# Linear attention with a gated convolution: batch 7's product of k and v moved next to the second half of batch 6's attention

## The chip, the cores and the metric

The kernel runs on one core of a Trainium2 chip. A core has a matrix engine (TensorE; PE in the rows, with its weight loads as PEld), VectorE (DVE), ScalarE (ACT), GpSimd (POOL), and SyncE (SP), from whose queue all transfers are issued here. Each engine works through its own queue in order; semaphores hold an instruction until what it reads is there and what it overwrites has been read. The metric is the time of one execution on the device, in microseconds, as the median of several runs.

## What is computed

For 8 batches of 576 tokens and 8 heads of 64 channels (512 channels in all), linear attention and then a gated convolution:

```python
q_s = exp(q - max(q, -1));  q_s = q_s / (sum(q_s, -1) + 1e-9)   # over a head's channels
k_s = exp(k - max(k, 2));   k_s = k_s / (sum(k_s, 2) + 1e-9)    # over tokens
kv = einsum('bhsd,bhse->bhde', k_s, v)
x = einsum('bhsd,bhde->bhse', q_s, kv)                          # heads side by side: 512 channels
gate = sigmoid(sum(conv_w[j] * shifted(x, 4 - j) for j in range(5)))
out = (gate * (x @ w_val)) @ w_out
```

## The kernel before

The 512 channels are four blocks of 128 partitions, and a block of one batch is a tile of 128 x 576. Each batch goes through the same steps. In the names, the first number is the batch and the second the block, and a letter says which engine does the step (a ScalarE, v VectorE, p GpSimd).

- Keys: `load_k` (SP), the maximum over tokens by `k_peak` (VectorE) from a copy in another layout (`load_km`), a way through DRAM that spreads it over the partitions (`k_row`, `k_spread`, both SP), then `k_sub b 0` to `b 4` subtract it and `k_exp`, `kt_exp` (ScalarE) take the exponential. `kv b` is 80 small matmuls; `kv_sums` and `kv_norm` (VectorE) divide by the sums.
- Queries: `q_max`, `q_sub`, `q_exp`, `q_total`, `q_log`, `l_turn` give the logarithm of the sum; `l_row` and `l_spread` (SP) send it through DRAM into the tile lb; `l_sub` subtracts it from the queries (qc) in the layout by channels and `c_exp` (ScalarE) gives the normalised queries.
- `attend b 0` and `attend b 1` are 8 + 8 matmuls each, and give blocks 0, 1 and 2, 3 of x in PSUM.
- Gate: `first` multiplies x by the last tap, `tap` (VectorE) adds another tap straight from PSUM, `far` (ScalarE) with `near` (GpSimd) does the same in two steps, `sigmoid` (ScalarE) is a tanh of half the sum.
- Products in float32 are made of two parts in the format fp32r, a high and a low one: `x_high`, `x_low` split x, and `g_high`, `g_low` split the gated value. `value b m` and `project b n` are then 24 matmuls each (three products, four blocks, two halves of the tokens). `gated` (VectorE) multiplies gate and value, `copy` takes a finished block out of PSUM (halved, by one or two engines), `put` (SP) sends it out.

What sets the order is the table `ORDER`, a list of steps written out in full; the loop at the end of the kernel issues them one by one, and each engine's queue is the table with the other engines' steps left out. The batches overlap: while the products of batch 5 run, the keys and queries of batches 6 and 7 are made ready. `HOMES` is a table beside it that says which buffer each new tile takes; its row `bank` is that of the four PSUM banks of the wide tiles (x, val, out, kv).

Of the kernel before, what the change touches and what calls it, by code (L numbers as in the profile page):

```python
# [90 lines left out]
    near 3 0 0, q_sub 5 0 p, near 3 1 0, x_low 3 2, load_k 5, load_qc 4 2, q_sub 5 3 p, tap 3 2 0, tap 3 3 2,
    load_v 7, copy 2 3 a a, far 3 2 1, l_sub 4 1 p, tap 3 2 2, kt_exp 4, value 3 0, far 3 3 1, sigmoid 3 1,
    load_km 7 0, q_exp 5 0 4, l_sub 4 0 p, value 3 1, near 3 2 1, sigmoid 3 0, tap 3 3 3, gated 3 0, k_spread 5,
    l_sub 4 3 p, kv 4, c_exp 4 1, q_total 5, g_high 3 0 a, load_km 7 1, put 2 2, c_exp 4 0, g_low 3 0 p, value 3 2,
    gated 3 1, load_q 6 0 5, near 3 3 1, kv_sums 4, q_log 5, load_v 5, kv_norm 4 v, load_qc 5 2, l_turn 5,
    sigmoid 3 2, value 3 3, tap 3 3 0, l_row 5, put 2 3, gated 3 2, sigmoid 3 3, g_high 3 2 a, g_high 3 1 p,
    g_low 3 1 p, k_sub 5 3 p, g_low 3 2 p, attend 4 0, gated 3 3, k_peak 7 0, g_high 3 3 a, x_high 4 0 v, load_qc 5 3,
    g_low 3 3 p, project 3 0, first 4 0 v, c_exp 4 3, tap 4 0 3, l_sub 4 2 p, far 4 1 1, load_km 7 3, tap 4 0 2,
    project 3 3, k_sub 5 0 p, tap 4 0 1, copy 3 0 a a, first 4 1 a, put 3 0, q_max 6 0 5, k_sub 5 4 p, l_spread 5,
    far 4 1 0, c_exp 4 2, k_sub 5 1 p, x_high 4 1 a, kt_exp 5, project 3 1, copy 3 3 a a, x_low 4 0, q_sub 6 2 p,  # L100
    tap 4 0 0, put 3 3, load_qc 5 0, k_sub 5 2 p, tap 4 1 3, tap 4 1 2, attend 4 1, x_low 4 1, copy 3 1 a a,
    near 4 1 1, k_exp 5, k_peak 7 3, project 3 2, q_sub 6 3 p, x_high 4 3 a, x_high 4 2 v, first 4 2 v, near 4 1 0,
    tap 4 2 3, first 4 3 a, tap 4 3 3, q_sub 6 4 p, x_low 4 2, sigmoid 4 0, q_sub 6 0 p, x_low 4 3, value 4 0,
    sigmoid 4 1, tap 4 3 2, q_sub 6 1 p, copy 3 2 a a, tap 4 2 2, put 3 2, l_sub 5 1 p, load_qc 6 1, kv 5, load_kt 6,
    gated 4 0, q_exp 6 0 5, k_row 6, l_sub 5 0 p, load_k 7, tap 4 2 1, g_high 4 0 p, value 4 2, c_exp 5 1, kv_sums 5,
    g_low 4 0 p, tap 4 2 0, c_exp 5 0, load_qc 6 0, kv_norm 5 v, load_km 7 2, k_peak 7 1, l_sub 5 3 p, load_k 6,
    k_spread 6, tap 4 3 1, sigmoid 4 2, tap 4 3 0, attend 5 0, gated 4 2, value 4 1, l_sub 5 2 v, first 5 1 a,
    load_q 7 0 5, x_high 5 0 a, tap 5 1 3, load_v 6, sigmoid 4 3, tap 5 1 2, g_high 4 2 v, tap 5 1 1, g_low 4 2 p,
    value 4 3, gated 4 1, x_high 5 1 a, g_high 4 1 p, x_low 5 1, tap 5 1 0, g_low 4 1 p, c_exp 5 2, c_exp 5 3,
    gated 4 3, first 5 0 a, far 5 0 3, g_high 4 3 a, g_low 4 3 v, project 4 0, far 5 0 0, near 5 0 3, near 5 0 0,  # L110
    q_total 6, attend 5 1, copy 4 0 a a, k_sub 6 1 p, put 4 0, project 4 2, load_qc 7 2, x_high 5 3 a, k_sub 6 2 p,
    tap 5 0 2, load_qc 6 3, first 5 2 a, put 3 1, x_low 5 0, far 5 2 3, tap 5 0 1, near 5 2 3, q_max 7 0 4,
    project 4 1, q_log 6, far 5 2 2, copy 4 2 a a, first 5 3 a, l_turn 6, q_sub 7 1 p, x_high 5 2 a, q_sub 7 0 p,
    x_low 5 3, l_row 6, copy 4 1 a a, x_low 5 2, value 5 1, q_sub 7 3 p, tap 5 3 3, q_sub 7 2 p, k_peak 7 2,
    sigmoid 5 1, l_spread 6, tap 5 3 2, sigmoid 5 0, near 5 2 2, project 4 3, gated 5 1, put 4 2, k_row 7,
# [5 lines left out]
    project 5 2, x_high 6 1 a, c_exp 6 3, l_row 7, k_sub 7 4 p, first 6 1 a, x_high 6 0 a, tap 6 1 3, k_sub 7 0 p,
    first 6 0 a, project 5 0, copy 5 2 a a, l_sub 6 2 v, kt_exp 7, put 5 2, l_spread 7, tap 6 0 3, k_sub 7 1 p,
    tap 6 0 2, k_sub 7 3 p, project 5 1, tap 6 0 1, copy 5 0 a a, c_exp 6 2, x_low 6 0, put 5 0, near 6 0 0,
    tap 6 1 2, tap 6 1 1, tap 6 1 0, attend 6 1, copy 5 1 a a, put 5 1, project 5 3, load_qc 7 0, x_high 6 2 a,
    x_high 6 3 v, far 6 2 2, k_sub 7 2 v, first 6 3 a, x_low 6 1, x_low 6 2, l_sub 7 3 p, x_low 6 3, value 6 1,
    sigmoid 6 1, tap 6 3 3, copy 5 3 a a, first 6 2 v, sigmoid 6 0, put 5 3, tap 6 2 3, near 6 2 2, k_exp 7,
    value 6 3, gated 6 1, l_sub 7 2 p, tap 6 3 2, tap 6 3 1, l_sub 7 1 p, tap 6 3 0, value 6 0, sigmoid 6 3,
    g_high 6 1 p, gated 6 3, g_low 6 1 p, tap 6 2 1, c_exp 7 2, tap 6 2 0, g_high 6 3 p, c_exp 7 1, l_sub 7 0 p, kv 7,
    sigmoid 6 2, value 6 2, kv_sums 7, kv_norm 7 v, c_exp 7 0, gated 6 0, g_low 6 3 v, g_high 6 0 a, g_low 6 0 p,
    attend 7 0, gated 6 2, g_high 6 2 a, x_high 7 1 v, first 7 0 a, g_low 6 2 p, project 6 1, c_exp 7 3, tap 7 0 3,  # L130
# [673 lines left out]
```

## Time and profile before

| | before |
|---|---|
| time, median of 3 runs | 287.67 us (287.59 to 287.77) |
| profiled execution: time | 287.65 us |
| profiled execution: span of the trace | 285.9 us |
| TensorE busy (matmuls) | 278.8 us, 98% |
| VectorE busy | 231.7 us, 81% |
| GpSimd busy | 205.8 us, 72% |
| ScalarE busy | 192.8 us, 67% |

The page names the share of each engine over the whole span. The windows say the same for a stretch: a row that gives as much busy time for TensorE as the stretch is long has no gap on TensorE in it. The chain of waits follows the work that ended last back from the end; pieces of the same engine that stand end to end in it have no wait between them. In the timeline the time in square brackets is how long an engine stood idle before the row, and what it waited for. A duration in a group of rows is a mean over the instructions of one line and one form.

### The profile page before, as it was taken

To read this page: it belongs to the slowest core of one execution; us is meant where nothing else is said; L and a number is where in the kernel's file an instruction comes from. 1 tells how busy PE (TensorE), PEld (TensorE's weight loads), DVE (VectorE), ACT (ScalarE), POOL (GpSimd) and SP (SyncE) were. 2 spreads that over 40 slices of the span, in tenths; PEclk is the share of its full clock that TensorE was granted. 3 is DMA by queue.
4 is the path that set the end of the run, shared out by engine and by line. 5 is a ranking of instruction groups with operands and counts; after the bars stand their busy time and mean duration, and the time that the engine had idled before them with its cause. 6 is when DMAs were issued, how large, how long until landed. Compare 5 with 4: busy or idle time off the path is not lost.

```text
span 285.9 us, 6653 instructions
## 1 busy us (share of the span) xinstructions
PE 278.8 (98%) x2640; PEld 250.6 (88%) x2640; DVE 231.7 (81%) x329; ACT 192.8 (67%) x322; POOL 205.8 (72%) x191
## 2 busy tenths in 40 slices
...
GB/s 241 397 414 399 316 226 301 214 416 346 84 262 345 250 284 128 332 198 224 371 417 257 211 225 322 287 165 126 153 182 159 217 0 2 44 41 85 0 83 85
DMA packets 23463, 62.93 MB, mean 220 GB/s; under 512 B 3432, under 2 KB 3976, under 8 KB 20744
## 3 DMA queue, kind: packets, MB, share of 16 engines
...
q14 instruction: 10, 0.08, 0.1%
HBM read 52.96 MB, written 9.54 MB: 219 GB/s over the span
## 4 chain that ended last, share of the span: by engine, by line
PE 84%; DVE 7%; ACT 2%; issue 1%; POOL 1%; DVEq 0%
PE val L630 36%; PE out_a L630 32%; PE kv L521 6%; PE x L580 5%; PE cv L676 2%; DVE gate L605 2%; DVE x L600 1%; PE qTps L546 1%; DVE e L292 1%; DVE kpk L340 1%; PE kps L387 1%; ACT q L506 1%; PE out_r L630 1%; PE out_l L630 1%; POOL f L295 0%
## 5 line engine op out<-in xcount | busy, mean ns | idle before, releaser
L630 PE MATMUL val<-x,w_val_hi 128*128 128x288 f32 x512 | 89.1, 295 | 0.1
L605 DVE SCALAR_TENSOR_TENSOR gate<-x,cw,gate 128x575 f32<-128x575 f32 (+3 forms) x98 | 78.8, 809 | 5.7 <-ACT gate L593 2.2
L630 PEld LDWEIGHTS val<-x,w_val_hi 128*128 128x128 f32 x512 | 75.3, 188 | 0.3 <-DVE x L600 0.3
L630 PE MATMUL val<-x,w_val_lo 128*128 128x288 f32 x256 | 56.1, 300 | 0.0
L630 PE MATMUL out_a<-gh,w_out_lo 128*128 128x288 f32 x248 | 54.6, 301 | 0.0
L630 PE MATMUL out_a<-gh,w_out_hi 128*128 128x288 f32 x248 | 53.2, 296 | 0.0
L697 POOL TENSOR_TENSOR gl<-g,gh 128x576 fp32r<-128x576 f32 x24 | 34.6, 1443 | 14.7 <-ACT gh L198 8.0
L630 PEld LDWEIGHTS out_a<-gh,w_out_lo 128*128 128x128 f32 x248 | 39.4, 188 | 5.7 <-issue 1.8
L630 PE MATMUL out_a<-gl,w_out_hi 128*128 128x288 f32 x248 | 43.0, 295 | 0.0
L614 POOL TENSOR_TENSOR gate<-gate,far 128x572 f32<-128x572 f32 (+3 forms) x22 | 29.1, 1324 | 18.7 <-DVE gate L605 10.0
L630 PEld LDWEIGHTS val<-x,w_val_lo 128*128 128x128 f32 x256 | 40.7, 188 | 1.6 <-DVE g L689 0.4
L630 PEld LDWEIGHTS out_a<-gh,w_out_hi 128*128 128x128 f32 x248 | 39.8, 188 | 0.0
L204 ACT ACTIVATE o<-out_a 128x576 f32<-128x576 f32 x27 | 17.6, 650 | 31.6 <-PE out_a L630 22.0
L630 PEld LDWEIGHTS out_a<-gl,w_out_hi 128*128 128x128 f32 x248 | 36.4, 188 | 0.0
L420 POOL TENSOR_TENSOR q<-q,qm 128x512 f32<-128x512 f32 x32 | 33.5, 1062 | 3.6 <-DVE qm L415 3.5
L689 DVE SCALAR_TENSOR_TENSOR g<-gate,val 128x576 f32<-128x576 f32 x32 | 23.8, 749 | 13.8 <-PE val L630 5.9
L490 POOL TENSOR_TENSOR qc<-qc,lb 128x576 f32<-128x576 f32 (+1 forms) x17 | 24.1, 1428 | 11.0 <-DMA lb<-lrow 11.0
L355 POOL TENSOR_TENSOR k<-k,kmax 128x512 f32<-128x512 f32 x23 | 30.2, 1330 | 0.2
L617 ACT ACTIVATE gate<-gate 128x576 f32<-128x576 f32 x30 | 20.2, 683 | 8.3 <-DVE gate L605 8.0
L600 DVE TENSOR_TENSOR x<-x,x 128x576 fp32r<-128x576 f32 x32 | 23.1, 749 | 1.7 <-ACT x L198 1.6
L610 ACT ACTIVATE far<-x,cw 128x572 f32<-128x572 f32 (+3 forms) x22 | 16.2, 737 | 9.2 <-PE x L580 4.0
L424 ACT ACTIVATE q<-q 128x512 f32<-128x512 f32 (+2 forms) x11 | 15.9, 1442 | 8.8 <-POOL q L420 8.8
...
## 6 DMA issues: line engine op xcount, KB each, us to landing
out<-o SPq DMA_DIRECT2D x31, 288.0 KB, 4.8
...
q<-in_q SPq DMA_DIRECT2D x7, 1024.0 KB, 10.5
km<-in_k_strided SPq DMA_DIRECT2D x24, 288.0 KB, 4.5
k<-in_k SPq DMA_DIRECT2D x6, 1024.0 KB, 7.4
qc<-in_q_channels SPq DMA_DIRECT2D x16, 288.0 KB, 5.0
...
kc<-in_k_channels SPq DMA_DIRECT2D x8, 288.0 KB, 8.5
```

What stands on the lines that cost most here:

```text
L204: nc.scalar.mul(out, in_, factor)
L355: engine(e).tensor_sub(kk[r, cs], kk[r, cs], mx[r, cs])
L420: engine(e).tensor_tensor(qq, qq, m, op=ALU.add if b < 2 else ALU.subtract)
L490: engine(e).tensor_sub(t, t, T["lb", b][:, p])
L521: nc.tensor.matmul(acc[h * D:(h + 1) * D, p, :], T["k", b][:, c, cs] if c < 4 else ktz[b % 2][:, cs], T["v", b][:, c, hd] if c < 4 else T[ ...
L600: nc.vector.tensor_sub(xl, T["x", b, p], T["xh", b, p].bitcast(F32))
L605: nc.vector.scalar_tensor_tensor(out=a, in0=x, scalar=w, in1=a, op0=ALU.mult, op1=ALU.add)
L614: nc.gpsimd.tensor_add(a, a, T["far", b, p, j])
L617: nc.scalar.activation(T["gate", b, p], T["gate", b, p], AF.Tanh, scale=0.5)
L630: nc.tensor.matmul(ps[:, cs], a[:, kb, ms], z[:, cs], start=(i == 0), stop=(i == len(parts) - 1))
L689: nc.vector.scalar_tensor_tensor(out=T["g", b, m], in0=T["gate", b, m], scalar=1.0, in1=T["val", b, m], op0=ALU.add, op1=ALU.mult)
L697: engine(e).tensor_sub(T["gl", b, m], T["g", b, m], T["gh", b, m].bitcast(F32))
```

## The change

The steps of `ORDER` from batch 3's second attention to batch 7's are put in another order, and `HOMES` deals out the buffers in the order in which the tiles now come. What each step computes is as before.

- `kv 7` stood between `value 6 0` and `value 6 2`. Now it stands between `project 5 0` and `attend 6 1`, with `kv_sums 7` behind it. `k_sub 7`, `k_exp 7` and `kt_exp 7` come before it, and `l_turn 7`, `l_row 7` come before attend 6 0.
- Of the products on TensorE, project 4 3 now comes before project 4 1, project 5 1 before 5 0, project 6 0 before 6 1, and value 6 0 before 6 3.
- 34 steps change the engine. From ScalarE to VectorE: 5 x_high, 3 first, 3 parts of copy, 2 g_high. From GpSimd to VectorE: 3 g_low, 3 k_sub (5 0, 5 1, 5 2), 2 l_sub (6 3, 7 2), 1 q_sub (7 3). From VectorE to ScalarE: 3 x_high, 1 g_high. From GpSimd to ScalarE: 3 g_high. From VectorE to GpSimd: l_sub 5 2, g_high 4 2, k_sub 7 2, g_low 6 3. From ScalarE to GpSimd: g_high 6 2.
- VectorE's queue from attend 4 0 to attend 5 0 has 30 instructions before and 37 now, from attend 6 0 to attend 6 1 it has 14 and 24.
- On SP's queue `load_v 7` and `load_km 7 0` go out sooner, `load_k 7` later (behind `k_spread 7`).

A row of the table in the diff:

```diff
-    g_low 5 0 v, put 4 3, l_sub 6 3 p, attend 6 0, gated 5 3, g_high 5 3 v, far 6 0 0, l_turn 7, g_low 5 3 p,
...
+    l_spread 7, project 5 0, tap 6 0 1, l_sub 7 2 v, k_sub 7 0 p, load_qc 7 3, k_sub 7 3 p, k_sub 7 1 p, l_sub 7 0 p,
+    k_exp 7, kv 7, kv_sums 7, put 5 2, copy 5 0 a a, c_exp 6 3, attend 6 1, first 6 3 v, tap 6 3 1, x_high 6 3 a,
```

TensorE's queue around kv 7, before. (A name is tile, batch, block and a buffer's number; x2 at the end is a count of like instructions, and rows that repeat are left out.)

```order
L630 MATMUL val_6_0_3184<-x2_6_2_3103,w_val_hi_77 128x288 x2
L630 MATMUL val_6_0_3184<-x2_6_3_3105,w_val_hi_77 128x288 x2
L521 MATMUL kv_7_3224<-v7_1903,k7_2398 64x65 x8
L521 MATMUL kv_7_3224<-vt6_1706,ktz1_84 64x65 x2
...
L521 MATMUL kv_7_3224<-v7_1903,k7_2398 64x65 x8
L521 MATMUL kv_7_3224<-vt6_1706,ktz1_84 64x65 x2
L630 MATMUL val_6_2_3266<-x2_6_0_2985,w_val_lo_78 128x288 x2
L630 MATMUL val_6_2_3266<-x2_6_0_2985,w_val_hi_77 128x288 x2
```

The same place on TensorE now:

```order
L630 MATMUL out_5_0_a_3030<-gh_5_3_2936,w_out_hi_79 128x288 x2
L630 MATMUL out_5_0_a_3030<-gl_5_3_2954,w_out_hi_79 128x288 x2
L521 MATMUL kv_7_3064<-v7_1786,k7_2878 64x65 x8
L521 MATMUL kv_7_3064<-vt6_1706,ktz1_84 64x65 x2
...
L521 MATMUL kv_7_3064<-v7_1786,k7_2878 64x65 x8
L521 MATMUL kv_7_3064<-vt6_1706,ktz1_84 64x65 x2
L580 MATMUL x_6_2_3112<-qT_6_2900,kvd_6_2884 64x288
L580 MATMUL x_6_3_3113<-qT_6_2900,kvd_6_2884 64x288
...
L630 MATMUL out_5_3_a_3138<-gh_5_1_2760,w_out_lo_80 128x288 x2
L630 MATMUL out_5_3_a_3138<-gh_5_1_2760,w_out_hi_79 128x288 x2
```

The 80 matmuls of kv 7 left the place between two value products and went between the last matmul of out 5 0 and the first of x 6 2.

VectorE's queue from gated 5 3 (the row that writes g 5 3) on, behind the start of attend 6 0, before:

```order
L689 SCALAR_TENSOR_TENSOR g_5_3_2939<-gate_5_3_2671,val_5_3_2890 128x576
L200 CAST gh_5_3_2941<-g_5_3_2939 128x576
L460 TENSOR_TENSOR lse1_82<-qm_7_2639,qs_7_2791 128x4x8
L465 STREAM_TRANSPOSE lt_7_2945<-lse1_82 32x32 x4
L605 SCALAR_TENSOR_TENSOR gate_6_1_2983<-x_6_1_2930,cw_76,gate_6_1_2983 128x575
L490 TENSOR_TENSOR qc_6_2_2919<-qc_6_2_2919,lb6_2723 128x576
L605 SCALAR_TENSOR_TENSOR gate_6_0_2989<-x_6_0_2929,cw_76,gate_6_0_2989 128x575
L605 SCALAR_TENSOR_TENSOR gate_6_0_2989<-x_6_0_2929,cw_76,gate_6_0_2989 128x574
L605 SCALAR_TENSOR_TENSOR gate_6_0_2989<-x_6_0_2929,cw_76,gate_6_0_2989 128x573
L600 TENSOR_TENSOR x2_6_0_2985<-x_6_0_2929,x2_6_0_2985 128x576
L605 SCALAR_TENSOR_TENSOR gate_6_1_2983<-x_6_1_2930,cw_76,gate_6_1_2983 128x574
L605 SCALAR_TENSOR_TENSOR gate_6_1_2983<-x_6_1_2930,cw_76,gate_6_1_2983 128x573
```

and now:

```order
L689 SCALAR_TENSOR_TENSOR g_5_3_2932<-gate_5_3_2609,val_5_3_2903 128x576
L697 TENSOR_TENSOR gl_5_2_2934<-g_5_2_2897,gh_5_2_2928 128x576
L200 CAST gh_5_3_2936<-g_5_3_2932 128x576
L595 TENSOR_SCALAR gate_6_0_2948<-x_6_0_2938,cw_76 128x576
L605 SCALAR_TENSOR_TENSOR gate_6_1_2950<-x_6_1_2939,cw_76,gate_6_1_2950 128x574
L605 SCALAR_TENSOR_TENSOR gate_6_0_2948<-x_6_0_2938,cw_76,gate_6_0_2948 128x574
L605 SCALAR_TENSOR_TENSOR gate_6_0_2948<-x_6_0_2938,cw_76,gate_6_0_2948 128x575
L200 CAST x2_6_0_2984<-x_6_0_2938 128x576
L208 TENSOR_SCALAR o_5_2_2986<-out_5_2_a_2956 128x576
L605 SCALAR_TENSOR_TENSOR gate_6_1_2950<-x_6_1_2939,cw_76,gate_6_1_2950 128x573
L605 SCALAR_TENSOR_TENSOR gate_6_1_2950<-x_6_1_2939,cw_76,gate_6_1_2950 128x572
L490 TENSOR_TENSOR qc_6_3_2791<-qc_6_3_2791,lb6_2870 128x576
```

Turning batch 7's sums (lse1, lt 7) went ahead of this place, and g_low 5 2, first 6 0, x_high 6 0, the copy of out 5 2 and l_sub 6 3 came into it.

GpSimd's queue from l_sub 6 0 on, up to the subtractions of batch 7's keys, before:

```order
L490 TENSOR_TENSOR qc_6_0_2437<-qc_6_0_2437,lb6_2723 128x576
L200 CAST gh_5_2_2884<-g_5_2_2880 128x576
L697 TENSOR_TENSOR gl_5_2_2888<-g_5_2_2880,gh_5_2_2884 128x576
L490 TENSOR_TENSOR qc_6_3_2629<-qc_6_3_2629,lb6_2723 128x576
L697 TENSOR_TENSOR gl_5_3_2951<-g_5_3_2939,gh_5_3_2941 128x576
L355 TENSOR_TENSOR kt6_2390<-kt6_2390,kmax_7_2829 64x512
L355 TENSOR_TENSOR k7_2398<-k7_2398,kmax_7_2829 128x512 x3
L614 TENSOR_TENSOR gate_6_0_2989<-gate_6_0_2989,far_6_0_0_2943 128x572
```

and now:

```order
L490 TENSOR_TENSOR qc_6_0_2513<-qc_6_0_2513,lb6_2870 128x576
L355 TENSOR_TENSOR kt6_2320<-kt6_2320,kmax_7_2874 64x512
L200 CAST gh_5_2_2928<-g_5_2_2897 128x576
L697 TENSOR_TENSOR gl_5_3_2954<-g_5_3_2932,gh_5_3_2936 128x576
L355 TENSOR_TENSOR k7_2878<-k7_2878,kmax_7_2874 128x512 x4
L490 TENSOR_TENSOR qc_7_0_3022<-qc_7_0_3022,lb7_3027 128x576
L490 TENSOR_TENSOR qc_7_1_3132<-qc_7_1_3132,lb7_3027 128x576
```

Two subtractions from qc and two g_low became l_sub 6 0, l_sub 7 0 and g_low 5 3; all four k_sub 7 of 128 x 512 are now here, and the first subtraction of batch 7's keys (kt6) comes ahead of g_high 5 2.

## Rows read from the trace of the kernel before

**Rows 1.** Windows: stretch, length, busy time per engine (instructions), TensorE clock, DMA share, GB/s.
```profile
148.80:173.40 24.60, 24.60 (x261) 22.76 (x260) 22.73 (x31) 15.79 (x21) 23.27 (x20) 1.00 0.76 241
173.40:210.70 37.30, 37.30 (x355) 35.51 (x354) 31.31 (x43) 26.73 (x36) 25.08 (x20) 1.00 0.68 219
210.70:221.60 10.90, 10.90 (x89) 10.13 (x88) 8.99 (x16) 6.17 (x10) 8.64 (x7) 1.00 0.46 122
```

**Rows 2.** Chain of waits around attend 6: start us, us, engine, instruction, count.
```profile
207.37 3.39 PE val L630 x24
210.76 1.13 PE x L580 x16
211.89 9.79 PE out_a L630 x72
...
226.21 9.60 PE val L630 x72
235.81 2.48 PE kv L521 x80
```

**Rows 3.** Timeline, weight loads at kv 7: start us, us, instruction, [idle time before].
```profile
235.74 0.55 PEld L521 LDWEIGHTS kv<-v,k 128*64 128x64 f32 x16 [0.16 <-issue]
```

**Rows 4.** Timeline of ScalarE (first) and VectorE (the rest), same columns.
```profile
227.42 1.91 ACT L359 ACTIVATE k<-k 128x2048 f32<-128x2048 f32 x1
...
210.90 0.76 DVE L689 SCALAR_TENSOR_TENSOR g<-gate,val 128x576 f32<-128x576 f32 x1 [1.39 <-POOL qc L490]
...
218.28 0.75 DVE L600 TENSOR_TENSOR x<-x,x 128x576 fp32r<-128x576 f32 x1
218.95 2.51 DVE L605 SCALAR_TENSOR_TENSOR gate<-x,cw,gate 128x574 f32<-128x574 f32 x3
```

**Rows 5.** Groups on GpSimd and ScalarE, 117.9 to 241.6 us: busy, mean ns; idle before.
```profile
L355 POOL TENSOR_TENSOR k<-k,kmax 128x512 f32<-128x512 f32 x15 | 19.9, 1343 | 0.2
...
L697 POOL TENSOR_TENSOR gl<-g,gh 128x576 fp32r<-128x576 f32 x13 | 18.6, 1432 | 11.5 <-ACT gh L198 5.1 <-DVE gh L200 4.5 <-DVE lse L460 1.5
...
L493 ACT ACTIVATE qT<-qc 128x576 f32<-128x576 f32 x15 | 9.9, 682 | 1.2 <-POOL qc L490 1.1
...
L359 ACT ACTIVATE k<-k 128x2048 f32<-128x2048 f32 x4 | 7.7, 1916 | 1.8 <-POOL k L355 1.8
...
L617 ACT ACT_TABLE_LOAD x3 | 3.8, 1283 | 0.1
```

**Rows 6.** Groups on VectorE, 117.9 to 241.6 us, same columns.
```profile
L600 DVE TENSOR_TENSOR x<-x,x 128x576 fp32r<-128x576 f32 x16 | 11.6, 749 | 0.1
...
L605 DVE SCALAR_TENSOR_TENSOR gate<-x,cw,gate 128x573 f32<-128x573 f32 x13 | 10.5, 809 | 0.2
...
L415 DVE TENSOR_REDUCE qm<-q 128x40 f32<-128x2560 f32 x1 | 2.8, 2810 | 0.0
...
L200 DVE CAST gh<-g 128x576 fp32r<-128x576 f32 x3 | 1.4, 453 | 0.0
...
L355 DVE TENSOR_TENSOR k<-k,kmax 128x512 f32<-128x512 f32 x1 | 0.7, 683 | 0.0
```

**Rows 7.** Transfers: k on the page; timeline of SP and of GpSimd behind lb 6.
```profile
k<-in_k SPq DMA_DIRECT2D x6, 1024.0 KB, 7.4
...
191.84 0.70 SPq L475 DMA_DIRECT2D lrow<-lt  x1
...
204.82 1.42 POOL L490 TENSOR_TENSOR qc<-qc,lb 128x576 f32<-128x576 f32 x1 [5.17 <-DMA lb<-lrow]
```

**Rows 8.** Timeline of GpSimd (three rows), then VectorE: neighbours reading SBUF.
```profile
207.46 1.43 POOL L697 TENSOR_TENSOR gl<-g,gh 128x576 fp32r<-128x576 f32 x1
208.85 1.94 POOL L490 TENSOR_TENSOR qc<-qc,lb 128x576 f32<-128x576 f32 x1
...
215.17 4.44 POOL L355 TENSOR_TENSOR k<-k,kmax 128x512 f32<-128x512 f32 x3
...
208.17 1.34 DVE L697 TENSOR_TENSOR gl<-g,gh 128x576 fp32r<-128x576 f32 x1
```

117 lines of the change are left out of this document (58 added, 59 removed).

## The prediction

> **What bounds the kernel now.** I read the busy time by stretches first. From 148.8 to 221.6 us TensorE is busy for 24.60 of 24.60, 37.30 of 37.30 and 10.90 of 10.90 us, at a granted clock of 1.00, the 2.4 GHz level [rows 1]. So in the stretch that the change rewrites nothing makes TensorE wait, and no wait can be won there; only TensorE's own work could get shorter. Beside it VectorE is busy for 22.73, 31.31 and 8.99 us [rows 1]: it has 1.9, 6.0 and 1.9 us left, and it is the engine that the change loads further.
>
> Then the chain of waits, which in this stretch is TensorE's instructions end to end [rows 2]. Three products of 24 matmuls that follow products take 9.60 us, or 3.20 each. The same three behind an attend take 9.79, and one behind a kv takes 3.39. So each return from the small matmuls of kv or attend to the wide ones costs 0.19 us. In the timeline the weight loads also stand idle for 0.16 us, for which the profile names only "issue", when kv begins [rows 3]. A kv itself is 2.48 us and an attend 1.13 [rows 2].
>
> **The change, part by part.**
>
> TensorE. No matmul is added or taken away. Kv 7 stood between two value products and now stands between project 5 0 and attend 6 1. Before, kv 7 and attend 6 1 each came out of wide products and went back into them; now the two make one island. That saves one return, 0.19 us, and at most the entry of 0.16 too: 0.19 to 0.35, and I take 0.27. The trace has no kv beside an attend, so the lower bound is zero (a rival below). The other exchanges (project 4 3 before 4 1, 5 1 before 5 0, 6 0 before 6 1, value 6 0 before 6 3) put like in the place of like: 3.20 for 3.20.
>
> What feeds kv 7. In the trace k_exp 7 ends at 227.42 + 1.91 = 229.33 [rows 4, 5], and kv 7 begins at 235.74 [rows 3]: 6.4 us to spare. They are spent now. Call T the start of attend 6 0's first matmul. Kv 7 is due at T + 1.13 + 9.79 = T + 10.92, attend 6 1 at T + 13.40.
> - The road to kv 7 begins with VectorE's gated 5 3, 0.2 us after T (210.90 against the chain's 210.76) [rows 4, 2]. Then come g_low 5 2, costed at the 0.75 of an x_low of the same shape, and g_high 5 3 (0.453) [rows 6]. A VectorE instruction that doesn't read its predecessor's result starts some 0.08 us before that one has ended (0.75 us at 218.28, the next at 218.95) [rows 4]. So g_high ends near T + 2.1. GpSimd then has g_low 5 3 at 1.43 and, in all, four k_sub 7 at 1.34 [rows 5], which with the overlaps ends near T + 8.7. K_exp 7 adds 1.91 [rows 5]: T + 10.6, with the handing over T + 10.7. The margin is 0.2 us.
> - The bank of attend 6 1's second block is freed by tap 6 0 1, which is the 17th VectorE instruction from gated 5 3 on: eight taps and firsts at 0.81, eight at 0.75, one at 0.453 [rows 6], 12.9 us, less some 1.0 of overlap: T + 12.2 against T + 13.40. The margin is 1.2 us.
> - Load_k 7 now stands on SP's queue behind the spread of kmax 7, which waits until the last k_sub 6 has read kmax 6. That is before k_exp 6, so some 1.9 us ahead of kv 6, and kv 6 starts 2.48 + 3.39 = 5.9 us ahead of T [rows 2]. From about T - 7.8 a load of k takes 7.4 us [rows 7], and GpSimd wants it near T + 3.4. That is 3.8 us to spare; I cost it at nothing, and at whatever exceeds 3.8 us if the cover goes.
>
> The 34 steps on another engine. VectorE gains 22 (13 from ScalarE, 9 from GpSimd) and gives up 8 (4 to each); 4 more go between the other two. By the rows it gains 3 firsts at 0.81, 14 steps near 0.75 (x_high, copy, g_low, l_sub, q_sub), 3 k_sub at 0.683 and 2 g_high at 0.453, 15.9 us, and gives up six at up to 0.75 and two at 0.453, 5.4 us [rows 6]: net some 10.5 us. What leaves GpSimd costs twice as much there (a k_sub 1.343, a g_low 1.432) [rows 5]. That relief of GpSimd and ScalarE is worth nothing by itself, since TensorE waits for neither. The dense place is from attend 4 0 to attend 5 0, 24.6 us of TensorE [rows 1], where VectorE goes from 30 to 37 instructions. Call U the start of attend 4 0. From gated 3 3 at U + 0.2 to kv_norm 5, which attend 5 0 needs at U + 24.6, stand 15 taps and firsts (12.1), nine instructions of 0.75 (6.7), one q_max of 2.81, two k_sub (1.4), one g_high (0.45) and the three short ones of kv 5, taken together at 1.3 (no more than g_high's each) [rows 6]: 24.8 us, less some 20 overlaps of 0.08, so U + 23.4. The margin is 1.2 us.
>
> What those sums leave out is that VectorE and GpSimd disturb each other, and the trace shows it. GpSimd's g_low runs from 207.46 for 1.43; VectorE's g_low, started beside it at 208.17, takes 1.34 and not 0.75; GpSimd's l_sub, started at 208.85 beside that, takes 1.94 and not 1.43 [rows 8]. Three k_sub beside VectorE's l_sub take 4.44 us and not 4.03 [rows 8, 5]. So a collision costs VectorE up to 0.59 and GpSimd 0.41 to 0.51. Taps, whose one input is x in PSUM, leave GpSimd at its ordinary times. The change takes the instructions with both inputs in SBUF (g_low, l_sub, k_sub, q_sub) on VectorE in this stretch from 8 to 13. Between T and the time at which kv 7 is due there are two such (g_low 5 2 and l_sub 6 3), and l_sub 6 3 runs right beside the four k_sub. One collision of 0.41 there against a margin of 0.2 makes kv 7 wait 0.2; none makes it wait not at all. I take 0.1 to 0.15.
>
> This is also where the Trainium skill speaks against the change: "SBUF — State Buffer", section "Who interferes with whom", says that a VectorE instruction with two SBUF inputs contends with a GpSimd instruction that reads SBUF, and that the later one blocks in full until the first is done. The trace agrees in kind and only partly in size: the late g_low lost 0.59 us where the whole rest of GpSimd's instruction, 0.72, was still to come. By that rule each collision would be priced by what is left of the other instruction, up to an estimated 1.4 us, and the sum would go to the first rival.
>
> Sum: 287.65 - 0.27 + 0.13 = 287.5, set against the profiled run's own time, 287.65, which is its span of 285.9 and 1.75 around it. The median of the runs is 287.67, so the two scales agree.
>
> **The rivals.**
>
> Slower: the margins are eaten by collisions and VectorE becomes the bound. The place is twofold, kv 7 with the bank behind it, and kv_norm 5 ahead of attend 5 0. For it: margins of 0.2, 1.2 and 1.2 us where the trace had 6.4 for k_exp 7; five more instructions that collide; VectorE with 1.9 us left out of 24.6 and work of 2.7 us added there. Against it: VectorE's idle time counts instructions that could have run earlier, and a wait at kv 7 covers one at the bank. It decides once the waits together exceed 0.27 + 0.6 = 0.87 us. Two collisions on the k_sub 7 (0.8) and four at U (4 x 0.59 - 1.2 = 1.2) give 287.38 + 2.0 = 289.4; the least that counts is 288.3. Price: 288.3 to 289.5.
>
> Lb 6 lands late. Its row of sums goes out after l_turn 6 and came back, in the trace, 13.0 us after the first of its transfers was issued at 191.84 (GpSimd's l_sub, which waited for it, began at 204.82) [rows 7]. In the new order 21 VectorE instructions stand between the end of l_turn 6 and gated 5 3: six taps, nine of 0.75, a q_total (at most q_max's 2.81) and five short ones, some 15.4 us with the overlaps [rows 6], and up to 3 more if VectorE waits between. So lb 6 lands between T - 5.4 and T - 2.4. Behind it come l_sub 6 0 (1.42 [rows 7]) and two c_exp at 0.68 [rows 5], 2.8 us: attend 6 0 has a margin of 2.6 us or is 0.4 late, and a table load of 1.28 on ScalarE [rows 5] can fall into it. L_sub 6 1 on VectorE waits for the same transfer and holds kv_norm 6 and g_low 5 2 behind it on its queue. A wait of 0.6 to 1.7 gives 288.0 to 289.1.
>
> The change doesn't do what it says: going from kv's 64 x 65 form to attend's 64 x 288 costs the same 0.19 as going to the wide ones. Then nothing is saved, and with up to 0.13 of waiting it is 287.65 to 287.8.
>
> Faster: with the full 0.35 saved and no wait it is 287.3, which is not yet 0.2%; more than that no row shows.
>
> **How the numbers follow.** 0.2% is 0.57 us, about what a measurement of this kernel can tell from no change: faster is below 287.1, slower above 288.25. My forecast, 287.5 (287.3 to 287.8), gets 0.55; no saving 0.12; collisions 0.19; a late lb 6 0.09, a third of it still within 0.2%; 0.05 is left for a gain that the rows don't show. So same is 0.55 + 0.12 + 0.03 = 0.70, slower 0.19 + 0.06 = 0.25, faster 0.05. The range goes from 287.2 to 288.7: out of it lie the gain, some two thirds of the collisions' case and a little of the late transfer's, somewhat under 0.2 in all.
>
> **What would show it.** Right: in the chain of waits kv 7 and attend 6 1 stand side by side and the product behind them takes 3.39, TensorE has no idle row before 282 us other than one of 0.1 to 0.2 at kv 7 put down to ScalarE's k_exp, and the stretch from attend 6 0 to the product behind attend 6 1 is 13.40 + 1.13 long. Wrong: a wait at attend 5 0 put down to VectorE's kv_norm or to ScalarE's c_exp; one at attend 6 0 put down to c_exp, with GpSimd's l_sub waiting for lb right before; a wait of over 0.4 us at kv 7, with k_sub 7 at over 1.5 us each beside VectorE's l_sub; or a pause of 0.19 between kv 7 and attend 6 1, which would mean that there was nothing to save.

## The result: slower by half a per cent

| | before | after |
|---|---|---|
| time, median of 5 runs | 287.77 us (287.59 to 287.91) | 289.36 us (288.83 to 290.01) |
| ratio | | 1.0056 (1.0040 to 1.0072) |
| profiled execution: time, span | 287.65, 285.9 | 288.83, 287.0 |
| VectorE busy | 231.7 | 242.4 |
| ScalarE, GpSimd busy | 192.8, 205.8 | 188.6, 196.6 |

The change costs 1.6 us. I had forecast 287.5, within 287.2 to 288.7. Two things are to be explained: that it is slower at all, and that its times spread over 1.2 us where those of the kernel before spread over 0.3. The profiled execution of after is the fastest of its five, so it shows only 1.2 of the 1.6 us.

The page of after, its span and its busy times:

```profile
span 287.0 us, 6652 instructions
...
PE 279.3 (97%) x2640; PEld 251.0 (87%) x2640; DVE 242.4 (84%) x343; ACT 188.6 (66%) x315; POOL 196.6 (68%) x184
```

VectorE has 10.7 us more to do, as worked out ahead (10.5), and GpSimd and ScalarE have less. The windows of after, for the three stretches of [rows 1], with the same columns:

```profile
149.00:173.90 24.90, 24.60 (x257) 22.73 (x256) 24.33 (x35) 13.61 (x21) 16.60 (x14) 1.00 0.77 211
173.90:211.30 37.40, 37.40 (x354) 35.57 (x353) 31.73 (x46) 30.14 (x41) 26.17 (x21) 1.00 0.67 197
211.30:222.80 11.50, 11.50 (x91) 10.34 (x92) 11.43 (x17) 5.08 (x6) 7.51 (x7) 1.00 0.85 204
```

TensorE, which was busy through all of them, has a gap of 0.30 us in the first. In the third it counts as busy throughout, but the stretch has become 0.6 us longer: waiting inside a series of matmuls is not a gap in this view. The chain shows both. After, around kv 5:

```profile
149.12 1.13 PE x L580 x16
150.25 9.81 PE out_a L630 x72
...
160.80 6.45 DMA out<-o
...
167.36 0.66 ACT o L204
...
168.06 2.55 PE kv L521 x80
...
174.01 1.13 PE x L580 x16
```

and from attend 6 0 to attend 7 0, which answers to [rows 2]:

```profile
211.34 1.68 PE x L580 x16
213.01 9.79 PE out_a L630 x72
222.81 2.48 PE kv L521 x80
225.29 1.39 PE x L580 x13
226.68 3.39 PE out_a L630 x24
...
242.87 1.13 PE x L580 x16
```

Set side by side, from the start of one attend to that of the next (before, the chain had attend 4 0 at 148.92, 5 0 at 173.44, 6 0 at 210.76 and 7 0 at 241.68):

| stretch | before | after | difference |
|---|---|---|---|
| attend 4 0 to attend 5 0, with kv 5 | 24.52 | 24.89 | +0.37 |
| attend 5 0 to attend 6 0 | 37.32 | 37.33 | +0.01 |
| attend 6 0 itself | 1.13 | 1.68 | +0.55 |
| attend 6 1 itself | 1.13 | 1.39 | +0.26 |
| the rest of attend 6 0 to attend 7 0, with kv 7 | 28.66 | 28.46 | -0.20 |

The sum is +0.99 us; 0.20 more was there before attend 4 0; in the second profile of the same kernel (experiment 5) attend 4 0 begins at 148.90, so this part comes and goes between executions. The last row is the gain that the change was to bring: kv 7 (2.48) stands between out 5 0 and attend 6 1, and one return to the wide products is gone. It is 0.19 to 0.20 us. The three rows above it are new waits, and the timeline of after names what was waited for (GpSimd, two rows, then ScalarE; at the end in brackets the idle time before a row and its releaser):

```profile
206.48 1.99 POOL L490 TENSOR_TENSOR qc<-qc,lb 128x576 f32<-128x576 f32 x1 [6.01 <-issue]
208.54 1.29 POOL L355 TENSOR_TENSOR kt<-kt,kmax 64x512 f32<-64x512 f32 x1
...
209.87 0.63 ACT L363 ACTIVATE ktz<-kt 64x512 f32<-64x512 f32 x1 [2.30 <-POOL kt L355]
210.51 1.26 ACT L493 ACTIVATE qT<-qc 128x576 f32<-128x576 f32 x2
...
224.22 0.65 ACT L204 ACTIVATE o<-out_a 128x576 f32<-128x576 f32 x1 [1.70 <-DMA out<-o]
224.76 0.68 ACT L493 ACTIVATE qT<-qc 128x576 f32<-128x576 f32 x1
```

GpSimd's l_sub 6 0 starts at 206.48 and takes 1.99 us beside VectorE's l_sub 6 1. The profile names no releaser for it ("issue"). I take its start as the landing of lb 6, because l_sub 6 1, which shares only lb with it, starts at 206.43, also after a wait. Behind it stands the subtraction for batch 7's tail of keys (kt), 1.29. On ScalarE kt_exp 7 (L363) waits 2.30 us for that one and holds up c_exp 6 0 and 6 1 (L493), which stand behind it and whose input is ready at 208.5. They end at 211.77, and attend 6 0, begun at 211.34, waits inside. At attend 6 1 the same pattern comes again: ScalarE's copy of out 5 0 at 224.22 waits 1.70 us until out 5 2 has been sent out of the buffer that it wants, and c_exp 6 3 stands behind that copy. At kv 5, in the chain, copy 3 2 waits for the transfer of out 3 1 (6.45 us), since both use one buffer; kv 5 needs the bank that this copy frees. In the row `o` of `HOMES` the new order gives buffer 0 to seven blocks in a row, from out 3 1 to out 5 2: buffer 1 is held by out 3 3 from its copy until `put 3 3`, which stands ahead of attend 6 0.

None of this is VectorE being late; its part is the 0.57 us that l_sub 6 0 loses beside it (1.99 in place of 1.42). My theory from here on: the loss is made by what stands ahead of what on ScalarE's and SP's queues, and by transfers whose time varies. The rival is the one that the prediction had put first: VectorE's load and its collisions with GpSimd.

### The profile page after: what moved, and what is told of

Its sections match the earlier page's. It is cut to its first block, busy times and chain, and to the rows that moved or that the text cites. A ratio compares the mean times of both kernels' runs of the same rounds, so it can differ in the third digit from the quotient of the medians.

```text
span 287.0 us, 6652 instructions
## 1 busy us (share of the span) xinstructions
PE 279.3 (97%) x2640; PEld 251.0 (87%) x2640; DVE 242.4 (84%) x343; ACT 188.6 (66%) x315; POOL 196.6 (68%) x184
## 4 chain that ended last, share of the span: by engine, by line
PE 81%; DVE 7%; ACT 2%; DMA 2%; issue 1%; POOL 1%; ACTq 0%; DVEq 0%
PE val L630 34%; PE out_a L630 31%; PE kv L521 6%; PE x L580 5%; DMA out<-o 2%; PE cv L676 2%; DVE gate L605 2%; DVE x L600 1%; PE qTps L546 1%; DVE e L292 1%; DVE kpk L340 1%; ACT q L506 1%; PE kps L387 1%; ACT o L204 1%; PE out_r L630 1%
## 5 line engine op out<-in xcount | busy, mean ns | idle before, releaser
L204 ACT ACTIVATE o<-out_a 128x576 f32<-128x576 f32 x24 | 15.6, 650 | 33.4 <-PE out_a L630 25.8
L697 POOL TENSOR_TENSOR gl<-g,gh 128x576 fp32r<-128x576 f32 x22 | 31.9, 1452 | 7.5 <-ACT gh L198 5.0
L490 POOL TENSOR_TENSOR qc<-qc,lb 128x576 f32<-128x576 f32 (+1 forms) x16 | 22.8, 1430 | 20.5 <-issue 11.6
L420 POOL TENSOR_TENSOR q<-q,qm 128x512 f32<-128x512 f32 x31 | 32.4, 1058 | 2.0 <-DVE qm L415 1.9
L355 POOL TENSOR_TENSOR k<-k,kmax 128x512 f32<-128x512 f32 x21 | 26.8, 1294 | 0.1
L415 DVE TENSOR_REDUCE qm<-q 128x8 f32<-128x512 f32 (+3 forms) x12 | 20.8, 1743 | 0.0
```

The source lines that it names most:

```text
L204: nc.scalar.mul(out, in_, factor)
L355: engine(e).tensor_sub(kk[r, cs], kk[r, cs], mx[r, cs])
L415: nc.vector.tensor_reduce(out=T["qm", b][:, cs], in_=qq, axis=AX.X, op=ALU.max, negate=b < 2)
L420: engine(e).tensor_tensor(qq, qq, m, op=ALU.add if b < 2 else ALU.subtract)
L490: engine(e).tensor_sub(t, t, T["lb", b][:, p])
L697: engine(e).tensor_sub(T["gl", b, m], T["g", b, m], T["gh", b, m].bitcast(F32))
```

## The experiments

Times are medians, with the ratio to the kernel before on the same chip and its interval. The first four kernels were run together, then four more, four more and three.

**1. kt_exp 7 behind c_exp 6 1.**

```diff
-    k_sub 7 4 p, kt_exp 7, l_turn 7, gated 5 2, l_row 7, c_exp 6 0, c_exp 6 1, value 5 3,
+    k_sub 7 4 p, l_turn 7, gated 5 2, l_row 7, c_exp 6 0, c_exp 6 1, kt_exp 7, value 5 3,
```

> The changed kernel with one step moved on ScalarE: kt_exp 7 goes behind c_exp 6 0 and c_exp 6 1. Queue theory (the extra 1.6 us is waiting that the new order of ScalarE's queue and of the output buffers makes): in the changed kernel attend 6 0 lasts 1.68 us in place of 1.13, because c_exp 6 0 stands behind kt_exp 7 on ScalarE, which waits 2.30 us for GpSimd's subtraction for kt. With kt_exp behind, attend 6 0 lasts 1.13 to 1.2. But k_exp 7 ended only 0.2 us ahead of kv 7, which is now due 0.5 earlier, so a wait of 0.2 to 0.4 shows at kv 7: the gain is 0.15 to 0.5 of the 0.55, 288.9 to 289.2 us where the changed kernel takes 289.36. VectorE theory (collisions and VectorE's load make the waits): nothing changes, 289.4, and attend 6 0 stays at 1.6 or more.

Measured: 288.28 us, 1.0023 (1.0011 to 1.0034). ScalarE's timeline:

```profile
208.54 1.26 ACT L493 ACTIVATE qT<-qc 128x576 f32<-128x576 f32 x2 [0.89 <-POOL qc L490]
209.92 0.63 ACT L363 ACTIVATE ktz<-kt 64x512 f32<-64x512 f32 x1
```

With lb 6 as late as before (l_sub 6 0 at 206.53) the two c_exp now end at 209.80 and attend 6 0 lasts 1.13 us. As foretold, the next in line came forward: out 5 0 took 3.44 us ahead of kv 7 in place of 3.29, a wait of 0.15 for k_exp 7. By the medians the exchange on ScalarE takes away about half of the loss (0.56 us are left of 1.6, or of 1.0 in the second session of after), but its interval overlaps that of the second session, 1.0024 to 1.0054. This profile, at 288.88, is one of the longer runs: project 3 0 was 0.39 us longer than before and attend 6 1 0.42. What the trace shows is that the wait at attend 6 0 is gone, and no step of VectorE was touched.

**2. The output buffers in turn, put 3 3 early.**

```diff
-    project 3 1, put 3 0, x_low 4 0,
+    project 3 1, put 3 0, put 3 3, x_low 4 0,
...
-    value 5 3, g_high 5 2 p, put 3 3,
+    value 5 3, g_high 5 2 p,
...
-    "o": "01010101101001000000010110100101",
+    "o": "01010101101001010101010110100101",
```

> The changed kernel with put 3 3 right behind put 3 0, and the two output buffers dealt out in turn from out 3 2 to out 4 1; in the changed kernel one of them is held by out 3 3 until put 3 3, some 45 us, and seven blocks go through the other one. Queue theory: copy 3 2 no longer waits for the transfer of out 3 1, kv 5 is not late by 0.36 us, and since transfers take different times from run to run, the spread of the times shrinks from 1.2 us (288.83 to 290.01) to under 0.6. Time 288.5 to 289.0. VectorE theory: 289.4, the same spread.

Measured: 292.67 us (289.34 to 294.39), 1.0151 (1.0113 to 1.0190); my expectation was wrong by 4 us. The wait at kv 5 did go (copy 3 2 ran at 165.49). But put 3 3 stood on SP's queue ahead of l_spread 5 and waited there for its copy, so lb 5 was issued at 158.16 and not 156.38, and l_sub 5 0, the last of GpSimd's three, ran 2.6 us later. Attend 5 0 waited 2.9 us, and that cost twice. The windows around it, and the first product's attend in TensorE's timeline:

```profile
174.00:176.00 2.00, 0.00 (x0) 0.00 (x0) 0.53 (x1) 0.49 (x1) 2.00 (x3) 0.96 0.94 329
176.00:178.00 2.00, 1.75 (x16) 0.80 (x16) 0.00 (x0) 1.91 (x4) 2.00 (x3) 0.50 1.20 287
178.00:180.00 2.00, 2.00 (x11) 1.63 (x8) 1.50 (x2) 0.74 (x1) 2.00 (x3) 0.50 0.80 287
180.00:182.00 2.00, 2.00 (x10) 2.00 (x10) 1.97 (x4) 1.84 (x3) 1.92 (x3) 0.50 0.51 201
182.00:184.00 2.00, 2.00 (x15) 2.00 (x14) 1.23 (x3) 1.61 (x1) 1.36 (x1) 0.84 0.76 250
```

```profile
176.25 2.20 PE L580 MATMUL x<-qT,kvd 64*64 64x288 f32 x16 [2.91 <-ACT qT L493]
```

TensorE had no matmul from 173.3 to 176.25. From about 176 on its granted clock is 0.50, the 1.2 GHz level, until some time between 182 and 184; the 16 matmuls of the attend take 2.13 us from start to start in place of 1.13, and the value product behind them 5.19 in place of 3.31. So 2.9 us of waiting were followed by half speed that cost another 2.9.

**3. Both, and c_exp 6 3 ahead of copy 5 0.**

```diff
-    k_exp 7, kv 7, kv_sums 7, put 5 2, copy 5 0 a a, c_exp 6 3, attend 6 1,
+    k_exp 7, kv 7, kv_sums 7, put 5 2, c_exp 6 3, copy 5 0 a a, attend 6 1,
```

> The changed kernel with kt_exp 7 behind c_exp 6 1, the output buffers as in the second kernel here, and c_exp 6 3 ahead of copy 5 0 on ScalarE (that copy waited 1.70 us for the transfer of out 5 2, and c_exp 6 3 behind it made attend 6 1 last 1.39 us in place of 1.13). Queue theory: the waits of 0.36, 0.55 and 0.26 us go and 0.2 to 0.4 comes at kv 7: 287.8 to 288.3 us. VectorE theory: 289.4.

Measured: 291.57 us, 1.0126 (1.0090 to 1.0162). Attend 6 0 and attend 6 1 lasted 1.13 us each, so both exchanges on ScalarE's queue do what they should; the stall at attend 5 0 from experiment 2 (value 4 2 took 6.21 us with its wait) hides it in the time. This profile's wait there, 2.74 us without a matmul, was not followed by half speed:

```profile
176.00:178.00 2.00, 1.70 (x20) 1.09 (x21) 0.45 (x1) 2.00 (x5) 2.00 (x3) 1.00 1.28 284
```

It is one of the shorter runs (290.47 of 289.53 to 292.77 us).

**4. One collision moved away.** L_sub 6 1 on VectorE goes behind kv_norm 6, so that it no longer runs beside GpSimd's l_sub 6 0.

> The changed kernel with one step moved on VectorE: l_sub 6 1 goes behind kv_norm 6, so that it no longer runs beside GpSimd's l_sub 6 0. This prices one collision on the way to attend 6 0. Queue theory with collisions as an ingredient: GpSimd's l_sub 6 0 takes 1.42 in place of 1.99, the chain l_sub 6 0, kt, kt_exp, c_exp ends 0.5 us sooner, attend 6 0 lasts 1.15 to 1.3, and 0.2 to 0.4 comes at kv 7: 289.0 to 289.3. If the collision costs nothing there: attend 6 0 stays at 1.6 or more, 289.4.

Measured: 288.61 us, 1.0035 (1.0020 to 1.0050). L_sub 6 0 took 1.43 us and not 1.99, but the subtraction for kt behind it, now beside l_sub 6 1, took 1.69 and not 1.29. From the start of l_sub 6 0 to the start of the c_exp it was 3.87 us, and 4.03 without the move: 0.16 us is what the collision is worth on this road, because the next instruction collides in its place. In this execution lb 6 landed 12.2 us after its issue, 1.3 later than in the first profile of after, so attend 6 0 waited longer all the same. The Trainium skill, "SBUF — State Buffer", section "Who interferes with whom", has the later of two such instructions block in full. In the first profile of after the GpSimd instruction, begun 0.05 us after VectorE's of 0.76, lost 0.57 of the 0.71 that were left; in [rows 8] it was 0.59 of 0.72. So the trace agrees in kind, and both times most of the rest was lost and not all of it.

**5. The changed kernel once more.**

> The changed kernel once more, unaltered, beside the others on one chip, with a second profile. Transfer theory (what differs from run to run, and makes the median 0.5 us longer than the profiled 288.83, is when lb 5, the row of sums for batch 5, lands, on which c_exp 5 0, 5 1 and attend 5 0 hang): 288.8 to 289.5 with a spread of over 1 us; in the profile either attend 5 0 begins at once, and then the time is near 288.8, or it waits, and the time is longer by that wait. VectorE theory: the same time, with the waits at kv 7 and attend 6 1 larger in the longer runs.

Measured: 288.65 us (288.14 to 289.52), 1.0039 (1.0024 to 1.0054). The chain of this second profile ahead of attend 6 0:

```profile
194.94 7.99 DMA lb<-lrow
...
206.93 2.01 POOL qc L490
...
209.00 1.29 POOL kt L355
...
210.32 0.63 ACT ktz L363
...
210.96 0.69 ACT qT L493
...
211.70 1.77 PE x L580 x16
```

The row of 7.99 us is one of the two transfers of lb 6. GpSimd's l_sub 6 0 and VectorE's l_sub 6 1 began at 206.93 and 206.88, and that is again taken as the landing of both. The road is the one of the first profile, but lb 6 landed 12.0 us after its issue and not 10.9. Attend 6 0 lost 1.52 us (0.95 before its first matmul, 0.57 inside), kv 5 only 0.06, attend 6 1 nothing. I had put the spread down to lb 5; it is lb 6 here, and the shares of the three places change from one execution to the next. The sum against the kernel before, 1.4 us, again agrees with the time.

**6 and 7. Lb 5 sooner, alone and with the other repairs.** L_row 5 goes ahead of load_km 7 2 (which holds SP until 153.4) and l_spread 5 ahead of put 3 0; the second kernel has the edits of experiment 3 as well.

> The changed kernel with two steps moved on SP's queue: l_row 5 ahead of load_km 7 2, which holds SP from 144.0 to 153.4 us there, and l_spread 5 ahead of put 3 0. Lb 5 is then issued some 2.5 us sooner than at 156.38. Transfer theory: it lands near 163.5 and not 166.0, attend 5 0 never waits, the spread shrinks and the median comes down by about 0.5, to 288.6 to 288.9; the waits at kv 5, attend 6 0 and 6 1 stay (1.2 us in all). VectorE theory: no change against the changed kernel.

> The changed kernel with four repairs: lb 5 sooner as in e5_lb5_sooner, put 3 3 early with the output buffers in turn, kt_exp 7 behind c_exp 6 1, c_exp 6 3 ahead of copy 5 0. With put 3 3 early alone the spread of lb 5 on SP's queue came 1.8 us later and attend 5 0 waited 3 us; here it stands ahead of both puts. Queue and transfer theory: all waits go except up to 0.2 at kv 7; kv 7 next to attend 6 1 saves 0.19: 287.4 to 287.9 us, with a spread under 0.6. VectorE theory: 289 or more.

Measured: 294.73 us, 1.0258 (1.0241 to 1.0275), and 293.75, 1.0213 (1.0199 to 1.0227). Wrong again, and instructive. The chain of the first:

```profile
153.49 0.61 SPq L486
...
154.85 9.90 DMA out<-o
...
164.86 0.66 ACT o L204
...
165.56 5.59 PE out_a L630 x24
```

Lb 5 did land 1.7 us sooner. But put 3 0 now stood right behind it, and the transfer of out 3 0, 288 KB, issued 1.4 us after lb 5, took 9.9 us; the page of before has 4.8 as the median of such transfers. Copy 3 1 wants the same buffer and waited 6.2 us, and project 3 2, which needs the bank, began 4.8 us late. It then took 5.59 us in place of 3.39, at a granted clock of 0.50 in the windows from 164 to 170. So this transfer, issued close behind the broadcast, landed with it: at 164.75, where GpSimd's l_sub 5 began on lb 5 at 164.35. The single output buffer isn't what made this wait: in the second kernel, which deals the buffers in turn, copy 3 1 still takes the one of out 3 0, and TensorE waited 5.3 us at the same place.

**8. The cause put into the kernel before: lb 5 later.** L_spread 5 behind put 3 3, 3.6 us later.

> The kernel before with one step moved: l_spread 5 behind put 3 3 on SP's queue, so that lb 5 is issued near 158.2 us and not 154.6. Nothing else is touched: VectorE, GpSimd and kv 7 are as before. Transfer theory: lb 5 lands near 168 to 169, GpSimd's l_sub 5 (at 166.8 before, with no wait) waits 1 to 2 us, attend 5 0 waits, and the time rises by 0.5 to 2.5 us with a spread of over 1 us: 288.2 to 290.2. VectorE theory: 287.7, as before.

Measured: 287.62 us, 0.9999 (0.9991 to 1.0008). No effect, and I had expected one. Lb 5 was needed in time for l_sub 5 at 166.7 in either case; issued at 158.19 it was there within 8.5 us. The kernel before has that much in hand; the changed one has not, since in experiment 2 lb 5 issued 1.8 us later made attend 5 0 wait.

**9. Load_k 7 out of lb 6's way.**

```diff
-    l_sub 6 0 p, k_spread 7, g_low 5 0 v, load_k 7, l_sub 6 1 v,
+    l_sub 6 0 p, k_spread 7, g_low 5 0 v, l_sub 6 1 v,
...
+    load_qc 7 2, load_k 7, x_high 5 3 a,
```

> The changed kernel with one step moved on SP's queue: load_k 7 (1 MB) goes behind load_qc 7 2, near 186.5 us, where the transfer engines are idle, and no longer at 200.9, while lb 6 is on its way. Transfer theory (the load of k for batch 7 runs beside lb 6 and delays it: lb 6 landed 10.9 and 12.0 us after its issue in the two profiles of the changed kernel, 9.9 in the kernel before): lb 6 lands about 10 us after its issue, attend 6 0 lasts 1.13 to 1.3 and the value product ahead of it 3.39, both without touching ScalarE's order; 287.8 to 288.3 us, against 288.65 of the changed kernel on this chip's kind of session, and a spread under 1 us. If only ScalarE's order counts: lb 6 as late as before, attend 6 0 at 1.7, 288.6.

Measured: 288.73 us, 1.0029 (1.0017 to 1.0041), no change against after. With the load at 186.53, lb 6 landed 10.8 us after its issue, and in three later kernels with the same edit 10.8, 11.5 and 12.0. So the load of k is not what delays lb 6. What does stays open: in the kernel before and its variants it was 8.3 to 9.9, in the changed order 10.8 to 12.2 wherever lb 6 left near 195. There qc 6 3 and out 4 3 leave right ahead of it, and in the kernel before nothing does; I did not test that.

**10. Put 3 3 behind lb 5.** As in experiment 2, but put 3 3 follows l_spread 5.

> The changed kernel with put 3 3 right behind l_spread 5 on SP's queue and the output buffers in turn from out 3 2 to out 4 1. Unlike the earlier placing ahead of lb 5, this delays lb 5 by nothing; out 3 3 goes out behind it and lands near 166. Queue theory: copy 3 2 finds its buffer free about a microsecond sooner than in the changed kernel, the wait of 0 to 0.36 us at kv 5 goes, attend 5 0 doesn't wait; nothing else changes: 288.3 to 288.7 us. Rival (any transfer near lb 5 delays it): attend 5 0 waits again, 289 to 292.

Measured: 289.29 us, 1.0050 (1.0034 to 1.0066). Attend 5 0 didn't wait, but kv 5 did, by 0.7 us: out 3 3 now went out behind lb 5 and landed at 167.6. Attend 6 0 lost 1.4 us, nearly as in experiment 5.

**11. Four repairs.** Experiments 1, 9 and 10, and c_exp 6 3 ahead of copy 5 0.

> The changed kernel with four repairs: load_k 7 near 186.5 us, put 3 3 behind l_spread 5 with the buffers in turn, kt_exp 7 behind c_exp 6 1, and c_exp 6 3 ahead of copy 5 0. Queue and transfer theory: no wait at attend 6 0, kv 5 and attend 6 1, at most 0.2 at kv 7, 0.19 saved by kv 7 next to attend 6 1: 287.4 to 287.8 us, a spread under 0.6. VectorE theory (its load and its collisions with GpSimd are what costs): 288.5 or more, since no step of VectorE has been touched.

Measured: 288.43 us, 1.0019 (1.0008 to 1.0031). The chain:

```profile
157.67 10.13 DMA out<-o
...
167.91 0.66 ACT o L204
...
168.61 2.55 PE kv L521 x80
...
211.88 1.13 PE x L580 x16
...
225.29 1.13 PE x L580 x16
```

Attend 6 0 and 6 1 are back at 1.13 us, out 5 0 ahead of kv 7 at 3.29. One wait is left, and it is the one that my buffer repair makes worse: out 3 3, issued at 157.67 behind lb 5, takes 10.1 us, and kv 5 begins 0.93 late.

**12. Load_k 7 late in the kernel before,** behind k_spread 7.

> The kernel before with the suspected cause put in: load_k 7 behind k_spread 7, so near 205 us and behind lb 6, as late in the order as in the changed kernel. In the kernel before, k_spread 7 itself waits until 205.4, when lb 6 has landed, so the load falls behind lb 6 and beside lb 7 instead. Transfer theory: lb 6 unchanged (lands about 10 us after issue), lb 7 and k 7 late; k_exp 7 has 6.4 us to spare there and attend 7 far more: 287.7, as before. If late loads of k cost by themselves: 288.2 or more.

Measured: 287.75 us, 0.9997 (0.9988 to 1.0005), as expected: with 6.4 us in hand at kv 7 the place of this load costs nothing.

**13. All repairs, batch 5's transfers in the order l_row 5, load_km 7 2, put 3 0, l_spread 5, load_qc 5 0, put 3 3.**

> The changed kernel with kt_exp 7 behind c_exp 6 1, c_exp 6 3 ahead of copy 5 0, load_k 7 near 186.5 us, and on SP's queue around batch 5: l_row 5 ahead of load_km 7 2, then put 3 0, l_spread 5, load_qc 5 0, put 3 3, with the output buffers in turn from out 3 2 to out 4 1. Lb 5 is issued near 155.1 and not 156.3, so out 3 3, behind it, lands near 165 and not 167.9. Buffer theory: copy 3 2 waits until 165 at most, kv 5 begins at once, no other wait is left: from attend 4 0 to kv 5 18.65 us, as in the kernel before, 0.19 saved at kv 7: 287.45 to 287.65 us, with a spread of 0.4. If transfers near lb 5 are the cause in another way: kv 5 or attend 5 0 waits 0.5 or more, 288.2 to 290.

Measured: 288.07 us (287.54 to 289.30), 1.0021 (1.0009 to 1.0033). Kv 5 waited 1.48 us in the profile: out 3 3, issued at 157.20, took 10.8 us. Sending lb 5 sooner did not bring the transfer behind it forward (it landed at 168.0, in experiment 11 at 167.8), and no repair of the buffers that I tried is better than the change's own single buffer.

**14. The repairs without the buffers:** kt_exp 7 behind c_exp 6 1, c_exp 6 3 ahead of copy 5 0, load_k 7 near 186.5; output buffers and puts as in the changed kernel.

> The changed kernel with kt_exp 7 behind c_exp 6 1, c_exp 6 3 ahead of copy 5 0 and load_k 7 near 186.5 us; puts and output buffers as in the changed kernel. Buffer theory: kv 5 waits for copy 3 2 and that for the transfer of out 3 1, 0 to 0.6 us from run to run; all else is gone: 287.6 to 288.1 us, a spread of 0.6. If kv 5's wait comes from something else, it is as in e10_four_repairs, 0.9, and the time 288.4.

Measured: 287.66 us (287.40 to 288.47), 1.0004 (0.9995 to 1.0014). This is the time of the kernel before, with all 34 changes of engine and VectorE as loaded as in after (241.8 us). When lb 6 landed, seen by GpSimd's l_sub 6 0, the two c_exp behind it on ScalarE, and the chain from attend 6 0 on:

```profile
206.84 2.00 POOL L490 TENSOR_TENSOR qc<-qc,lb 128x576 f32<-128x576 f32 x1 [7.07 <-issue]
...
208.88 1.26 ACT L493 ACTIVATE qT<-qc 128x576 f32<-128x576 f32 x2 [1.99 <-POOL qc L490]
```

```profile
210.63 1.13 PE x L580 x16
211.76 9.79 PE out_a L630 x72
...
221.57 2.55 PE kv L521 x80
224.12 1.13 PE x L580 x16
225.25 3.39 PE out_a L630 x24
...
241.44 1.13 PE x L580 x16
```

Lb 6 was as late as in the second profile of after (11.98 us after its issue), where attend 6 0 lost 1.52 us; here the two c_exp end at 210.14, 3.30 us after the landing, and attend 6 0 lost nothing. Kv 5 began at once as well (copy 3 2 at 165.49, right behind k_exp 5 on ScalarE, with no wait for its buffer), and kv 7 waited 0.08. From attend 4 0 to attend 7 0 it is 92.66 us, 92.76 in the kernel before: 0.19 saved, 0.08 given back. The profiled run is the fastest of the eleven. Some take as long as 288.47 us, which the single buffer would explain, but no trace of such a run is here.

**15. One output buffer in the kernel before.** Put 3 3 goes ahead of attend 6 0, the blocks from out 3 1 to out 5 2 go through the other buffer, put 3 1 follows its copy.

> The kernel before with one cause put in: put 3 3 goes ahead of attend 6 0, so that out 3 3 holds one of the two output buffers, and the blocks from out 3 1 to out 5 2 go through the other; put 3 1 follows its copy at once. Buffer theory: copy 3 2 waits for the transfer of out 3 1, issued near 160.6, which lands behind lb 5 some 4 to 6.5 us later, and kv 5 waits 0 to 0.8 us: 287.8 to 288.5 us, with more spread than the 0.3 of the kernel before. If the buffers are no cause: 287.7, no wait at kv 5.

Measured: 298.45 us, 1.0378 (1.0364 to 1.0391). The cause was dosed wrongly, and the place was another one than I had said: copy 3 2 waited 0.44 us without holding up kv 5, but further on

```profile
192.51 1.38 DMA lrow<-lt
...
195.64 7.67 DMA out<-o
203.42 0.66 ACT o L204
204.12 4.94 PE out_a L630 x24
```

put 4 2 stands on SP's queue behind l_row 6 and l_spread 6, so out 4 2 leaves at 195.64, the next copy waits for it until 203.42, and TensorE for that copy's bank: 8.9 us. The product that waited then took 4.94 us, at a granted clock of 0.50 from 198 to 206. It shows what a single buffer does where a put stands late on the queue, not what it costs at kv 5.

## Why the prediction was wrong, point by point

**What bounds the kernel, and the gain.** Right. TensorE had no wait to lose, and only its own work could shrink. One return to the wide products was saved at 0.19 us; of my 0.19 to 0.35 the lower end holds, and the entry of 0.16 is not saved (I had taken 0.27).

**Kv 7's road.** Right in size, and in part by luck. I had k_exp 7 end 0.2 us ahead of kv 7; it did so by 0.22 in the profile of after, where attend 6 0's wait had pushed kv 7 back by 0.55, and once that wait was gone it came 0 to 0.15 late (experiments 11, 14 and 1), where I took 0.10 to 0.15. But I had charged that to a collision on the four k_sub 7, and these took 5.07 us in experiment 14, 1.27 each, none of them slowed. What used up the margin there is that gated 5 3, behind l_sub 6 2 on VectorE's queue, began 0.54 us after attend 6 0 and not 0.2. The bank of attend 6 1 and load_k 7 were in time, as costed.

**VectorE's load and the collisions.** I gave this 0.19 as the likeliest way to be slower. It fell: the steps on VectorE are all still in experiment 14, and its time is that of the kernel before. Collisions took place at nearly the price given (0.57 us on l_sub 6 0, with 0.41 to 0.51 expected; 0.63 on l_sub 6 3 beside the k_sub 7, with up to 0.59 expected), but moving one away gave 0.16.

**Lb 6.** Here the prediction failed. The rival had the right place and the right landing (4.9 us ahead of attend 6 0 in the profile, I had said 2.4 to 5.4), and the sign that I had named for it came, but the step "behind it come l_sub 6 0 and two c_exp, 2.8 us" left out two instructions which the new order puts between them: k_sub 7 4 on GpSimd, 1.29, and kt_exp 7 on ScalarE, 0.63, ahead of c_exp 6 0. With them and the collision it is 5.3 us (206.48 to 211.77), more than the 4.9. So what I had priced as a margin of up to 2.6 was a wait of 0.55, or 1.5 where lb 6 came a microsecond later, and the chance of 0.09 should have been the largest of all. I had read GpSimd's and ScalarE's queues for kv 7 and not for attend 6 0, though kt_exp 7 is one of the steps moved.

**The output buffers.** Not in the prediction at all. I had taken the row `o` of `HOMES` as bookkeeping. It makes copy 3 2 wait for out 3 1 (0 to 0.4 us at kv 5) and copy 5 0 for out 5 2 (with c_exp 6 3 behind it, 0 to 0.65 at attend 6 1).

**The sum.** 287.65 + 0.37 + 0.55 + 0.26 - 0.19 = 288.64; the profiled run was 288.83, the rest being the 0.20 ahead of attend 4 0. The median of that session, 289.36, lies higher because the profiled execution was its fastest, and what the other four lost is in no trace; the second session had 288.65. Experiments 1 and 14 account for the loss: one exchange on ScalarE leaves 0.6 us of it, two exchanges (with load_k 7 moved, which had no effect of its own that could be measured) leave none that can be measured. The second exchange was not run alone. What makes lb 6 land later than before, and what the single buffer costs by itself, stays open.

No version is shown to beat the kernel before: the 0.1 us that experiment 14's chain gains is less than a measurement can tell.

## What to carry to other kernels

When an order is rewritten, follow every chain into each step that the bottleneck waits for, on all the queues that it passes, and not only into the step that was moved: an unrelated instruction that waits at the head of an in-order queue (here an exponential for the next batch, or a copy that lacks a buffer) hands its wait to what stands behind it. Buffer assignments belong to the order: a step that holds one of two buffers turns the rest into a chain of transfer times, and these vary from run to run. A saving of 0.2 us on the bottleneck is not worth spending margins of several microseconds that cover such variation.

## What the runs showed of the chip

- A transfer of 288 KB that was issued 1.4 to 2.8 us behind a broadcast of two times 576 KB (that of lb 5) landed 9.9 to 10.8 us after its issue (experiments 6, 11, 13), and one issued 1.7 us ahead of such a broadcast kept no copy waiting in the changed kernel.
- After a wait of 2.9 us TensorE's matmuls came back at granted clock 0.50, the 1.2 GHz level, for some 6 us, which cost as much again as the wait itself (experiment 2). After waits of 4.8 and 8.9 us the clock was 0.50 too, and the product behind cost some 2.1 and 1.6 us more (experiments 6 and 15). After a wait of 2.7 us it was 1.00 (experiment 3).
- The same broadcast, that of lb 6, landed 8.3 to 12.2 us after its issue, depending on the order around it and, with the same kernel, on the execution (10.9 and 12.0).
